# The opening of a block-sparse attention kernel: identity transposes on TensorE between the turns, the masks' flags ahead of the scores, second products chunk by chunk

## The chip, the cores and the metric

The kernel runs on one core of one Trainium2 chip. The metric is the device time of one execution in microseconds (us). Five timed executions of the kernel before took 645.33, 646.21, 646.53, 649.99 and 654.07 us; their median is 646.53 us. The changed kernel is timed against the kernel before on the same chip, and the result is told as a ratio with an interval.

## What is computed

The program is two layers, one after the other. The first is BigBird attention: 4 batches, 8 heads, 768 rows, head dimension 64, in blocks of 32 rows. A query block sees its neighbours, the first and the last block, and three sampled blocks; the queries of the first and the last block see everything. The second is a dropless mixture of experts over the 3072 resulting rows.

```python
scores = scale * np.matmul(q, k.transpose(0, 1, 3, 2))
mask = np.abs(blk_i - blk_j) <= window            # window = 1, in blocks of 32
mask = mask | (blk_i == 0) | (blk_j == 0) | (blk_i == n_blocks - 1) | (blk_j == n_blocks - 1)
for qb in range(n_blocks):
    for kb in sampled_blocks[qb]:
        mask[qb * block:(qb + 1) * block, kb * block:(kb + 1) * block] = True
...
x = attention output, (3072, 512)
expert = argmax(x @ w_gate); y = relu(x @ w1[expert]) @ w2[expert]; out = gate weight * y
```

## The kernel before, in words

All data are float32. The change touches only the opening, before the loop over steps of attention begins (L425 to L436); the rest of the kernel is the same.

**Loads.** SyncE (SP) issues its DMAs in program order. First come eight loads (L293, by `fill_rows`, L146): k and q of batch 0 for the four pairs of heads, each with rows on the partitions. Pairs 0 and 1 land in two staging slots of the tile `room`, pairs 2 and 3 in `kr`. Then come the six 128-row chunks of v (L295, L164). Each chunk that has landed is stored again, all heads of a row side by side, into a DRAM tensor `v_rows` (L297 and L298, L170), because the sampled blocks of v are later gathered from there, row by row.

**Lists.** `make_lists` (L187 to L263) builds small tables from the sampled blocks on GpSimd (POOL) and VectorE (DVE): `spread` and `whose` say which block belongs to which query tile, `own` which half of the partitions counts. At its end TensorE (PE) transposes the identity 22 times into a PSUM tile `idle` that nobody reads (L261 and L262).

**Turns.** `turn_rows` (L148 to L157) brings k or q of one pair into the form that scores need, head dimension on the partitions: 12 transposes of 64x64 on TensorE into a PSUM tile, and then four copies out of it, two on ScalarE (ACT) and two on DVE. `turn_first(pr)` does k and q of one pair, so the opening has eight turns.

**Scores.** `scores_first(pr)` (L422) multiplies the 64 queries of the first and last block with all keys of pair `pr`: 24 products of 64x64 (L351, two matmul records each) and one exponential on ACT (L361).

**Flags and masks.** `make_masks` (L265 to L280) multiplies `spread` and `whose` into a PSUM tile `fl` (four products, L269), from which DVE makes `rows_of` (L270), the row numbers that the gathers read, and four pieces of `mask` (L276).

**Second products.** `attend_all` (L402) multiplies the exponentials with v: for one pair, six chunks and two heads, 12 products into a PSUM bank (L405, by `product`, L385). The order before is pair by pair: pair 0 with chunks 0 to 5, then pair 1, and so on.

**PSUM.** The pool `ps_s` has three buffers of two banks, handed out in rotation to the turns (`tp`), the scores (`s`), `idle` and, before, `fl`. The pool `ps_o` has two buffers of one bank for the second products, one for pairs 0 and 1, one for pairs 2 and 3. A new user of a buffer waits until the last reader of the one before is done.

**Order.** Instructions are issued by hand: on each engine they run in the order in which the code names them. Behind the opening come, before and in the first pass of the loop over steps (L1289 on): `fetch_ends` (SP, reads of `v_rows`, L529), two gathers of v rows (POOL, `fetch_values`, L519, by `rows_of` out of `v_rows`), `place_keys`, `place_middle` and `place_values` (copies on ACT and DVE, L561, L545, L546, L538, L539), the scores of the first two steps (L351, L356), their masks (`masked_two`, L371), and then the second products of the first step (`attend_last`, L407), whose values are in the tile `around` that the gathers and reads fill. SP goes on with the loads of batch 1's k and q into the staging slots (`fill_next`, L140).

The order of the opening before:

```python
    turn_first(0)
    turn_first(1)
    scores_first(0)
    turn_first(2)
    scores_first(1)
    turn_first(3)
    make_masks(*lists)
    make_lists_pool.close()
    scores_first(2)
    scores_first(3)
    for pr in range(NPR):
        attend_all(0, pr, es[("all", pr)], range(NCH))
```

Of the kernel before, what the change touches and what calls it, by code (L numbers as in the profile page):

```python
# [7 lines left out]
F32 = mybir.dt.float32  # L8
# [9 lines left out]
def kernel(  # L18
# [11 lines left out]
    nc = tc.nc  # L30
    P = 128
# [4 lines left out]
    NCH = S // P  # L36
    CW = NCH // 2 * P
    NPR = H // 2
# [32 lines left out]
    ident = const.tile([P, P], F32, name="ident")  # L71
# [12 lines left out]
    ps_o = ctx.enter_context(tc.tile_pool(name="ps_o", bufs=2, space=PSUM))  # L84

    upper, lent = {}, ExitStack()
# [11 lines left out]
    NTI = NB // 2 - 1  # L98
# [49 lines left out]
    def turn_rows(b, pr, which, src):  # L148
        tp = upper["ps_s"].tile([P, 2, 512], F32, name="tp", tag="s")
        for hh in range(2):  # L150
            r = slice(hh * D, (hh + 1) * D)
            for j in range(KG // 2):
                nc.tensor.transpose(tp[:, hh, j * D : (j + 1) * D], src[r, j * P : (j + 1) * P], ident[r, r])
        for hh, copy in enumerate((nc.scalar.copy, nc.vector.tensor_copy)):
            to = sets[b][which][hh * D : (hh + 1) * D, pr, :].rearrange("p (i j a) -> p a i j", j=KG // 2, a=2)
            for a in range(2):
                copy(to[:, a], tp[a * D : (a + 1) * D, hh, : KG // 2 * D].rearrange("p (j i) -> p i j", i=D))  # L157
# [104 lines left out]
            nc.tensor.transpose(idle[:, 0, :P], ident[:], ident[:])  # L262
        return spread, whose, own, qb  # L263

    def make_masks(spread, whose, own, qb):  # L265
        fl = upper["ps_s"].tile([P, 2, 2, NTI], F32, name="fl", tag="s")
        for w in range(2):
            for ch in range(2):
                nc.tensor.matmul(fl[:, w, ch, :], lhsT=spread[:, w, ch, :], rhs=whose[:], start=True, stop=True)  # L269
        nc.vector.tensor_scalar(  # L270
            rows_of.rearrange("p (t c) -> p c t", c=2), fl[:, 0], scalar1=float(BLK), scalar2=qb[:, 2:3], op0=ALU.mult, op1=ALU.add,
        )
        for ch, p0 in ((0, D), (1, 0)):
            for ti in range(2):
                shape = [P - p0, NG - ti, 2, BLK]
                nc.vector.tensor_tensor(  # L276
                    mask[p0:, : NG - ti, 1 + ch, ti, :].rearrange("p t (a i) -> p t a i", a=2),
                    fl[p0:, 1, ch, ti::2].unsqueeze(2).unsqueeze(3).to_broadcast(shape),
                    own[p0:, ch, :].unsqueeze(1).unsqueeze(3).to_broadcast(shape), op=ALU.mult,
                )  # L280
# [9 lines left out]
    for n in range(2 * NPR):  # L290
        pr, which = n // 2, n % 2
# [9 lines left out]
    lists = make_lists(make_lists_pool.enter_context(tc.tile_pool(name="mk", bufs=1)))  # L301
    rt = {}
    xbs, xos, lgs, banks_of, es = {}, {}, {}, {}, {}
# [26 lines left out]
    def plan_all(b, pr):  # L330
        kT = sets[b][0][:, pr, :]
        return [(j, at_cols(kT, c * P + j * D, D), all_queries(b, pr), c * D, D) for c in range(NCH) for j in range(2)], []
# [11 lines left out]
    def scores(*plans):  # L344

        ss = [upper["ps_s"].tile([P, 2, 512], F32, name="s") for _ in plans]
        for s, (few, _) in zip(ss, plans):
            for j, keys, queries, a, n in few:
                for hh in range(2):
                    r = slice(hh * D, (hh + 1) * D)  # L350
                    nc.tensor.matmul(s[j * D : (j + 1) * D, hh, a : a + n], lhsT=keys(r), rhs=queries(r), start=True, stop=True)  # L351
        for s, (_, many) in zip(ss, plans):
            for keys, queries, a, n in many:
                for hh in range(2):
                    r = slice(hh * D, (hh + 1) * D)
                    nc.tensor.matmul(s[:, hh, a : a + n], lhsT=keys(r), rhs=queries(r), start=True, stop=True)  # L356
        found = []
        for s in ss:
            e = ea[:, units[0] % NE, :].rearrange("p (h w) -> p h w", h=2)
            units[0] += 1  # L360
            nc.scalar.activation(e, s[:, :, : 6 * D], AF.Exp, scale=scale)  # L361
            found.append(e)
        return found
# [18 lines left out]
    def product(b, g, pr, ti, hh, e, values, last):  # L382
        bank, begun = bank_of(b, g, pr)
        op = bank[:, : 4 * (D + 4)].rearrange("p (r h w) -> p r h w", r=2, h=2)
        nc.tensor.matmul(  # L385
            op[ti * D : (ti + 1) * D, pr % 2, hh, : D + 1], lhsT=e, rhs=values[:, (2 * pr + hh) * VW : (2 * pr + hh + 1) * VW],
            start=ti not in begun, stop=last, skip_group_check=True,
        )
        begun.add(ti)
# [12 lines left out]
    def attend_all(b, pr, e, chunks):  # L402
        for c in chunks:
            for hh in range(2):
                product(b, GL, pr, 1, hh, e[:, hh, c * D : (c + 1) * D], sets[b][2][:, c, :], c == NCH - 1)  # L405
# [9 lines left out]
            attend_all(b, pr, e_all, range(3, NCH))  # L415


    def turn_first(pr):
        for which in range(2):
            turn_rows(0, pr, which, first[(pr, which)])  # L420

    def scores_first(pr):  # L422
        (es[("all", pr)],) = scores(plan_all(0, pr))

    turn_first(0)  # L425
    turn_first(1)
    scores_first(0)
    turn_first(2)
    scores_first(1)
    turn_first(3)  # L430
    make_masks(*lists)
    make_lists_pool.close()
    scores_first(2)
    scores_first(3)
    for pr in range(NPR):
        attend_all(0, pr, es[("all", pr)], range(NCH))  # L436
    wp = ctx.enter_context(tc.tile_pool(name="wp", bufs=1))
    sm = ctx.enter_context(tc.tile_pool(name="sm", bufs=1))
    work = ctx.enter_context(tc.tile_pool(name="work", bufs=2))
# [864 lines left out]
    for i, (b, g, half) in enumerate(steps):  # L1304
# [15 lines left out]
        if two:  # L1320
            b_, g_, _ = steps[i + 1]
# [245 lines left out]
```

## Time and profile before

| | us |
|---|---|
| median of five timed executions | 646.53 |
| the profiled execution, its own time | 652.5 |
| its span from the first to the last instruction | 650.8 |
| TensorE busy in the span | 616.0 (95%) |
| VectorE busy | 303.7 (47%) |
| ScalarE busy | 223.6 (34%) |
| GpSimd busy | 183.7 (28%) |
| mean granted TensorE clock | 0.965 of full |

Times in the profile count from the start of the span. PE is TensorE's matmul side, PEld its weight loads, DVE VectorE, ACT ScalarE, POOL GpSimd, SP SyncE; a q behind the name is the engine's queue, which issues DMAs. A row of the timeline gives start, duration, engine, line, operation, output<-input and count, and in brackets how long the engine sat idle before it and what ended that. PEclk in a table by stage is the clock that was granted to TensorE, as a share of full speed. The end of a matmul is modelled, so a row's duration reaches some 0.2 us past the time at which the next can start.

The opening and the first steps fill the first 45 of the 650.8 us. In that stretch the granted clock is at half in two spells, 11.47 to 21.71 and 31.95 to 42.19 us.

### The profile page before, as it was taken

What the parts mean: (1) busy time and instruction counts of PE and PEld (TensorE: products, weight loads), DVE (VectorE), ACT (ScalarE), POOL (GpSimd) and SP (SyncE); (2) the same over time, 40 slices, a digit from 0 to 9 for tenths busy, and PEclk for the clock granted to TensorE, in tenths of its full rate; (3) what the DMA queues carried; (4) which work ended last, traced back from release to release, by engine and by line L of the source; (5) the groups of instructions that cost most, each with busy time, mean ns of one, the idle gap of its engine ahead of it and who ended that gap; (6) DMA issues with size and microseconds to landing.
All of it is one profiled execution on the core that took longest, in us unless ns stands there. A gap on an engine that the chain in (4) does not pass through costs nothing. (4 is left out here: it accounts for less than half of the span.)

```text
span 650.8 us, 21378 instructions
## 1 busy us (share of the span) xinstructions
PE 616.0 (95%) x8952; PEld 516.4 (79%) x8952; DVE 303.7 (47%) x978; ACT 223.6 (34%) x430; POOL 183.7 (28%) x288
## 2 busy tenths in 40 slices
PE   7899989989999998899999999999989999999995
PEld 7898889888989887798677777777869678867862
DVE  6547655765667498634920385202091024702200
ACT  5547755765767553431111011111111111111110
POOL 2246733543455244710111221011400212020210
PEclk8879999999999996989999999999999999999998
DMA  9889976896787337966888999869995799989950
GB/s 267 212 179 247 261 187 136 209 263 170 173 194 232 96 107 261 305 235 208 326 307 298 321 382 348 306 227 381 396 398 199 237 406 395 349 277 405 397 190 20
DMA packets 125065, 170.93 MB, mean 263 GB/s; under 512 B 71236, under 2 KB 71237, under 8 KB 124934
## 3 DMA queue, kind: packets, MB, share of 16 engines
q1 hardware_dynamic: 114896, 137.61, 64.9%
q0 software_dynamic: 10000, 31.59, 15.3%
q8 instruction: 80, 1.31, 0.8%
q14 instruction: 51, 0.42, 0.2%
q10 hardware_dynamic: 38, 0.00, 0.0%
HBM read 150.11 MB, written 19.33 MB: 260 GB/s over the span
## 5 line engine op out<-in xcount | busy, mean ns | idle before, releaser
L1127 PEld LDWEIGHTS hp<-around,room 128*128 128x128 f32 x1216 | 138.3, 192 | 7.3 <-issue 5.1
L1127 PE MATMUL hp<-around,room 128*128 128x128 f32 x1216 | 140.8, 276 | 1.4 <-ACT kr L1134 1.4
L1108 DVE STREAM_TRANSPOSE around<-xg 32x128 f32<-32x128 f32 x208 | 62.9, 303 | 126.4 <-PE hp L1127 95.9
L519 POOL DMA_INDIRECT around<-v_rows,rows_of x88 | 96.8, 1100 | 62.7 <-issue 25.2
L361 ACT ACTIVATE ea<-s 128x768 f32<-128x768 f32 x104 | 80.0, 810 | 95.4 <-PE s L356 85.9
L1141 PE MATMUL zp<-room,kr 128*128 128x512 f32 x256 | 112.7, 594 | 0.0
L385 PE MATMUL op<-around,ea 128*64 128x65 f32 x2112 | 92.7, 232 | 11.2 <-DMA around<-v_rows,rows_of 9.2
L385 PEld LDWEIGHTS op<-around,ea 128*64 128x64 f32 x2112 | 80.5, 144 | 20.4 <-DMA around<-v_rows,rows_of 10.7
L1141 PEld LDWEIGHTS zp<-room,kr 128*128 128x128 f32 x256 | 47.5, 190 | 54.6 <-issue 54.6
L367 DVE TENSOR_TENSOR ea<-ea,mask 128x768 f32<-128x768 f32 x80 | 73.3, 955 | 17.4 <-ACT ea L361 16.7
L1134 ACT ACTIVATE kr<-hp 128x512 f32<-128x512 f32 x36 | 21.5, 597 | 117.3 <-PE hp L1127 109.9
L1156 POOL DMA_INDIRECT out_dram<-kr,sB x14 | 14.1, 1006 | 164.9 <-ACT kr L1146 106.1
L1146 ACT ACTIVATE kr<-zp,xg 128x512 f32<-128x512 f32 x16 | 11.0, 687 | 101.2 <-PE zp L1141 101.2
L1234 DVE STREAM_TRANSPOSE ea<-ea 32x128 f32<-32x128 f32 x84 | 21.7, 285 | 32.5 <-DMA ea<-x_rows,gB 31.8
L356 PE MATMUL s<-other,kr 64*128 64x64 f32 x352 | 27.5, 272 | 1.1 <-issue 1.1
L1156 POOL DMA_INDIRECT out_dram<-kr,sA x5 | 5.1, 1019 | 82.8 <-ACT kr L1146 70.6
L356 PE MATMUL s<-room,kr 64*128 64x64 f32 x352 | 26.4, 266 | 0.2 <-issue 0.2
L356 PEld LDWEIGHTS s<-other,kr 64*128 64x128 f32 x352 | 25.6, 201 | 0.0
L356 PE MATMUL s<-other,xk 64*128 64x128 f32 (+1 forms) x192 | 23.3, 320 | 2.4 <-issue 2.4
L351 PE MATMUL s<-room 64*64 64x64 f32 x736 | 24.6, 243 | 0.3 <-DVE room L157 0.3
L356 PEld LDWEIGHTS s<-room,kr 64*128 64x128 f32 x352 | 24.5, 194 | 0.4 <-issue 0.4
L351 PE MATMUL s<-other 64*64 64x64 f32 x736 | 22.5, 228 | 0.4 <-DVE cnA L777 0.4
(344 smaller groups left out, 853.2 us busy)
## 6 DMA issues: line engine op xcount, KB each, us to landing
room<-in_moe_w_dram SPq DMA_DIRECT2D x46, 2048.0 KB
room<-in_moe_w_dram SPq DMA_DIRECT2D x16, 512.0 KB
x_rows<-xb SPq DMA_DIRECT2D x20, 256.0 KB
room<-in_k_dram SPq DMA_DIRECT2D x24, 192.0 KB
room<-in_q_dram SPq DMA_DIRECT2D x24, 192.0 KB
v_rows<-room SPq DMA_DIRECT2D x12, 260.0 KB
v_rows<-other SPq DMA_DIRECT2D x12, 260.0 KB
other<-in_v_dram SPq DMA_DIRECT2D x16, 192.0 KB
```

Of the source, the lines that this page charges most:

```text
L351: nc.tensor.matmul(s[j * D : (j + 1) * D, hh, a : a + n], lhsT=keys(r), rhs=queries(r), start=True, stop=True)
L356: nc.tensor.matmul(s[:, hh, a : a + n], lhsT=keys(r), rhs=queries(r), start=True, stop=True)
L361: nc.scalar.activation(e, s[:, :, : 6 * D], AF.Exp, scale=scale)
L367: nc.vector.tensor_tensor(e, e, m[:, None, :].to_broadcast([P, 2, 6 * D]), op=ALU.mult)
L385: nc.tensor.matmul(op[ti * D : (ti + 1) * D, pr % 2, hh, : D + 1], lhsT=e, rhs=values[:, (2 * pr + hh) * VW : (2 * pr + hh + 1) * VW], sta ...
L519: nc.gpsimd.indirect_dma_start(out=around[p0:, par, 1 + ti + 2 * ch, :], out_offset=None, in_=v_d[b][:, :], in_offset=bass.IndirectOffsetO ...
L1108: nc.vector.transpose(xT[d, :, t], xg[t, :DM].rearrange("p (c q) -> p c q", c=DB)[:, :, d])
L1127: nc.tensor.matmul(hp[:, m, :], lhsT=st[i]["w1"][:, c, fb * P : (fb + 1) * P], rhs=st[i]["xT"][:, c, :], start=(c == 0), stop=(c == DB - 1),)
L1134: nc.scalar.activation(hT[:, g * (FB // 2) : (g + 1) * (FB // 2), :], hp[:], AF.Relu)
L1141: nc.tensor.matmul(zp[:], lhsT=st[i]["hT"][:, fb, :], rhs=st[i]["w2"][:, fb, :], start=(fb == 0), stop=(fb == FB - 1),)
L1156: ins = nc.gpsimd.indirect_dma_start(out=to[:, :], out_offset=bass.IndirectOffsetOnAxis(ap=at, axis=0), in_=rows, in_offset=None, bounds_c ...
L1234: nc.vector.transpose(xT_u[d, :, j * P + tq * 32 : j * P + (tq + 1) * 32], xg_u[t, j, :DM].rearrange("p (c q) -> p c q", c=DB)[:, :, d],)
```

## The change

A function `keep_busy(n)` transposes the 128x128 identity `n` times on TensorE, into a PSUM bank `idle_bank` that nobody reads. It is called behind each of the eight turns, with 2, 3, 11, 4, 4, 4, 4 and 4 transposes, and with 10 between the scores of pairs 2 and 3: 46 in all. The four flag products leave `make_masks` and become `make_flags`, which runs ahead of the first scores and writes into a buffer of `ps_o` and no longer of `ps_s`; DVE makes the masks from it at the same place as before. The second products go chunk by chunk: chunk 0 for all four pairs, then chunk 1, and so on. On ACT, DVE, POOL and SP the same instructions stand in the same order as before; only TensorE's order differs.

```diff
-    def make_masks(spread, whose, own, qb):
-        fl = upper["ps_s"].tile([P, 2, 2, NTI], F32, name="fl", tag="s")
+    def make_flags(spread, whose):
+        fl = ps_o.tile([P, 512], F32, name="op")[:, : 4 * NTI].rearrange("p (w c t) -> p w c t", w=2, c=2)
         for w in range(2):
             for ch in range(2):
                 nc.tensor.matmul(fl[:, w, ch, :], lhsT=spread[:, w, ch, :], rhs=whose[:], start=True, stop=True)
+        return fl
+
+    def make_masks(fl, own, qb):
...
+    idle_bank = ps_o.tile([P, 512], F32, name="op")
+
+    def keep_busy(n):
+
+        for _ in range(n):
+            nc.tensor.transpose(idle_bank[:, :P], ident[:], ident[:])
+
     def turn_first(pr):
         for which in range(2):
             turn_rows(0, pr, which, first[(pr, which)])
+            keep_busy(WHILE[2 * pr + which])
+
+    WHILE = (2, 3, 11, 4, 4, 4, 4, 4)
...
     turn_first(0)
     turn_first(1)
+    flags = make_flags(*lists[:2])
     scores_first(0)
     turn_first(2)
     scores_first(1)
     turn_first(3)
-    make_masks(*lists)
+    make_masks(flags, *lists[2:])
     make_lists_pool.close()
     scores_first(2)
+    keep_busy(10)
     scores_first(3)
-    for pr in range(NPR):
-        attend_all(0, pr, es[("all", pr)], range(NCH))
+    for c in range(NCH):
+        for pr in range(NPR):
+            attend_all(0, pr, es[("all", pr)], (c,))
```

## The prediction, on record before the changed kernel ran

> **What bounds the kernel now.** I read the page first, then the clock by stage, then the timelines of TensorE, GpSimd and SyncE over the first 45 us, because the change touches nothing behind. From the page, two lines:
>
> ```profile
> PE 616.0 (95%) x8952; PEld 516.4 (79%) x8952; DVE 303.7 (47%) x978; ACT 223.6 (34%) x430; POOL 183.7 (28%) x288
> L385 PE MATMUL op<-around,ea 128*64 128x65 f32 x2112 | 92.7, 232 | 11.2 <-DMA around<-v_rows,rows_of 9.2
> ```
>
> TensorE is the busy engine, and most of the little that its second products wait for is a gather of v rows (9.2 of 11.2 us). So a gain in the opening has to show as TensorE starting real work earlier. TensorE's timeline of the opening:
>
> ```profile
> 1.59 4.09 PE L262 MATMUL idle<-ident 128*128 128x128 f32 x22 [1.59 <-POOL ident L73]
> ...
> 8.83 0.74 PE L153 MATMUL tp<-ident,room 64*128 64x64 f32 x12 [0.49 <-DVE room L157]
> 9.88 0.93 PE L351 MATMUL s<-room 64*64 64x64 f32 x48 [0.31 <-DVE room L157]
> ...
> 16.99 1.88 PE L269 MATMUL fl<-whose,spread 24*128 24x11 f32 x8
> 18.79 2.84 PE L351 MATMUL s<-room 64*64 64x64 f32 x96
> 21.56 5.87 PE L385 MATMUL op<-room,ea 128*64 128x65 f32 x96
> ...
> 30.82 0.45 PE L385 MATMUL op<-around,ea 128*64 128x65 f32 x4 [0.53 <-DVE ea L371]
> 32.97 2.43 PE L385 MATMUL op<-around,ea 128*64 128x65 f32 x20 [1.70 <-DMA around<-v_rows,rows_of]
> ```
>
> The last row is the one that decides: with everything of the opening done, TensorE sits idle for 1.70 us, until a gather has landed just before 32.97. What sets that gather's time? GpSimd's timeline, and SyncE's for the stores that it reads behind:
>
> ```profile
> 25.45 1.17 POOL L519 DMA_INDIRECT around<-v_rows,rows_of  x1 [19.66 <-DMA around<-v_rows]
> 26.93 0.93 POOL L519 DMA_INDIRECT around<-v_rows,rows_of  x1 [0.30 <-issue]
> ```
> ```profile
> 16.79 0.43 SPq L164 DMA_DIRECT2D room<-in_v_dram  x1
> 17.86 3.92 SPq L170 DMA_DIRECT2D v_rows<-room  x3
> ```
>
> The gathers are issued at 25.45 and 26.93 behind a wait for DMAs on `v_rows`, whose last stores SyncE issues from 17.86 to 21.78, each when its chunk of v has landed. `rows_of`, the other thing that they need, DVE had ready at 19.69 (L270 starts at 19.44 and takes 0.24). No TensorE instruction is in this chain: loads, v chunks, stores, gathers. Then the clock, by stages that follow its steps (columns: PE, PEld, DVE, ACT, POOL busy, then PEclk):
>
> ```profile
> 4.65:8.06 3.41, 2.56 (x44) 2.29 (x43) 2.76 (x16) 1.59 (x4) 0.98 (x5) 1.00 1.00 306
> 8.06:11.47 3.41, 2.27 (x74) 1.94 (x72) 3.29 (x6) 3.01 (x6) 0.00 (x0) 1.00 1.05 390
> 11.47:14.89 3.42, 3.21 (x71) 2.82 (x68) 2.04 (x5) 2.20 (x5) 0.00 (x0) 0.50 1.21 228
> ...
> 18.30:21.71 3.41, 3.41 (x100) 3.26 (x101) 3.32 (x9) 0.82 (x2) 0.00 (x0) 0.50 1.15 321
> ...
> 28.54:31.95 3.41, 2.20 (x42) 1.78 (x40) 2.14 (x5) 3.01 (x6) 1.14 (x2) 1.00 1.23 256
> 31.95:35.37 3.42, 2.40 (x24) 2.28 (x24) 0.20 (x1) 0.75 (x4) 2.32 (x4) 0.50 1.28 215
> ...
> 38.78:42.19 3.41, 3.41 (x40) 3.29 (x39) 1.92 (x2) 2.20 (x6) 0.01 (x1) 0.50 0.66 169
> 42.19:45.61 3.42, 3.42 (x90) 3.15 (x89) 2.18 (x7) 1.63 (x3) 1.60 (x4) 1.00 0.43 87
> ```
>
> The clock goes to half behind a stage in which TensorE was busy 2.27 of 3.41 us (67%), and again behind one with 2.20 (64%); behind 2.56 (75%) it stayed. Both times it comes back 10.2 us later. The first spell lies under the wait at 32.97; in the second, TensorE has work throughout and pays.
>
> **The change part by part.** Durations are start to start, so the 0.2 us of modelled tail drops out.
>
> *Fillers, 46.* The 22 identity transposes give the price: 14 starts from 1.59 to 4.63 are 217 ns each, those behind it 109 ns. I take 109 ns at full clock, 217 at half, so 5.0 us in all. Five lie before the turn of pair 1's k, which waits for its load until 7.60 anyway: nothing. If that load came earlier, they would cost 0.5.
>
> Do transposes hold the clock up? Row: their spacing halves at 4.63 with nothing but transposes issued before, so they raised it. The Trainium skill ("TensorE: Matmul & The Clock Gate", Part 4) says that the full clock does not engage for transposes, because they do not count as TensorE work in the same way; by it the fillers only cost, and the sum would be that of the second rival, 648.9. The row is of this very instruction, and I follow it.
>
> *Until pair 2's k turn* (11.15 before). Turn of k1 at 7.60 (0.58), 11 fillers (1.20) to 9.38, turn of q1 (0.58), 4 fillers (0.44) to 10.40, flags now here (8 records of 107 ns, half their 213 in the slow stretch: 0.86) to 11.26, scores of pair 0 (0.74) to 12.00. The pauses of 8.83, 9.88 and 11.15 are gone, and this point is 0.85 later.
>
> *From there to the second products* (21.56 before, at half clock). Four turns 2.3, three scores 2.2, 26 fillers 2.8: 19.4. DVE's 16 copies of 557 ns and ACT's of 498 ns with four exponentials of 0.81 keep up, since the fillers fill what they leave. The last exponential ends about 20.4.
>
> *Second products.* A new wait: pair 2's bank held the flags, so its first product waits for DVE's four mask pieces (1.94 us behind the copies, done near 19.9; 21.65 before), and pair 3's for its exponential. Behind them queue all other second products, and behind those the scores of step 0. With some 0.4 us of this and 96 records of 58 ns (5.6) they end at 25.4, against 27.36. If the masks were no earlier than before they would end at 27.3, still not late. Chunk 5 of v, stored from 21.46, is needed near 24.4: no wait; pair by pair it would have been wanted at 20.
>
> *Flags and masks early.* `rows_of` and the masks come some 1.5 us earlier on DVE. Nothing waits for them: the gathers wait for the stores. SyncE's and GpSimd's queues hold the same instructions, and none of those up to the second gather depends on the moved ones. Gathers four and five (32.35, 33.63) may go up to 2 us earlier, queued behind the second; nothing waited for them in the trace. They cost nothing, or, if they slow the second, at most 1.2 us, the spacing of two gathers on their queue (26.93 to 28.16).
>
> *What is late next.* Step 0's scores take 25.4 to 28.3 (2.93 as before), its first second products come 3.46 behind their start, at 28.9, and then TensorE waits for the same gather until 32.97: 3.9 us where it was 1.7. The 2 us saved become waiting. The path's sum: 0.
>
> *The clock behind the wait.* The longer pause puts the clock at half before 32.97 whatever the stages' edges are. Before, the edge was at 31.95; an execution whose edge falls up to 1.9 us behind 32.97 ran that long at full clock and no longer does, which is half of it, 0 to 0.9, and 0.3 on the mean. From both sides: if the second spell went (TensorE arriving so late that it hardly waits), 9.22 us at half would become 4.7, by 60 ns against 118 ns a record of L385 (5.80 us for 96, 2.36 for 20): 4.5 gained. If the before of the timed runs had no such spell and the changed one has, 4.5 lost. I take 0.3, near the row of the profile, in which both have it.
>
> The Trainium skill (same page, "Why this matters for your kernels") asks for no pauses over about 3 us. By it the 1.7 us before are harmless and the 3.9 us are not, and the sum would be 651.0. The row says that 0.53 and 1.70 us close together were enough to lose the clock.
>
> *Sum.* In the profiled execution, 652.5 + 0.3 = 652.8. It stands 6.0 above the median; its 41 us of half clock before 643 are more than every execution need have. On the median, 646.5 + 0.3 = **646.8**.
>
> **Rivals.** *Second spell gone, faster.* If copies or masks hold TensorE so that it arrives at 31 to 32 with the clock up, it keeps it. For: 2 to 3 us of delays would do. Against: the sum is 28.9. Price 4.5: 642.3.
>
> *Fillers at half clock, slower.* If the clock falls at 11.47 all the same, 26 fillers cost 217 ns each, 5.6; with 0.85 from above, less 1.88 for the flags that left the slow stretch, TensorE arrives at 30.82 + 4.6 = 35.4, 2.4 behind the gather: 648.9. It decides from a delay of 2.15 us on, about 15 slow fillers. Against: the pauses that cost the clock are filled. This is the one that says that the change does not do what it does on its face.
>
> *The pause costs the clock that the timed runs before had, slower.* Place 32.97, price up to 4.5: 651.0. For: the profile is 6.0 over the median. Against: in any position of a 3.41 us stage, one holds at least 1.1 us of the two pauses, as the one that lost it did (1.2).
>
> **How the numbers follow.** Forecast 0.72 (644.5 to 648.5 by the scatter of the three middle runs), spell gone 0.06, slow fillers 0.08, clock lost 0.14. The range takes in the last two and most of the scatter, 643.0 to 651.0. A measurement of this kernel tells about 1% from no change: below 640.1 or above 653.0. No case reaches either; I leave 0.04 and 0.06 for what I have not seen, and 0.90 for the same.
>
> **What would show it.** Right: full clock from 11.47 to 21.71, second products starting near 19.4 and ending near 25.4, the gathers issued at 25.4 and 26.9 as before, and a TensorE wait of 3 to 4 us that ends near 32.97 by the gather. Wrong: the first gather issued before 25, which would mean that its wait was for something the change moves; or full clock at 33, or TensorE arriving behind the gather.

## The result, and the profile after

The changed kernel took 651.95 us at the median of 51 executions (641.67 to 660.67), the kernel before 649.99 us at the median of 93 (642.60 to 659.37). That is 1.96 us more, a ratio of 1.0030; the means differ by 1.84 us, with a standard error of 0.58. The ratio, made as for every kernel below, is 1.0002, with a 95% interval of 0.9984 to 1.0021: it takes only the executions within 1.5% of the fastest of their own kernel, 21 of the 51 and 71 of the 93, and the one execution at 641.67 us puts that bar at 651.3 us for the changed kernel, against 652.2 for the kernel before. By either reading there is no gain, and a loss of at most some 0.5%. The profiled execution of the changed kernel took 651.54 us, of which the span is 649.8, at a mean granted clock of 0.976. That clock is higher than the 0.965 of before, and the time is no better. The question is where the clock went.

From the page (busy us, share, instructions; then one costly group; then the queue that brings instructions):

```profile
PE 618.6 (95%) x8998; PEld 517.4 (80%) x8998; DVE 304.0 (47%) x978; ACT 222.9 (34%) x430; POOL 185.4 (29%) x288
...
q8 instruction: 81, 1.33, 0.9%
...
L388 PE MATMUL op<-around,ea 128*64 128x65 f32 x2112 | 92.3, 233 | 8.9 <-DMA around<-v_rows,rows_of 8.1
```

The 46 transposes are there (8998 less 8952). They are 92 instructions, since each matmul has its weight load beside it, and the instruction queue reads one packet more than before (81, before 80). The wait for gathered v rows is 8.1 us over the whole run, where it was 9.2.

TensorE's timeline of the opening (start, duration, engine, line, operation, output<-input, count, and the idle time ahead of it with what ended it):

```profile
8.63 1.42 PE L426 MATMUL op<-ident 128*128 128x128 f32 x11
...
11.27 1.05 PE L269 MATMUL op<-whose,spread 24*128 24x11 f32 x8
12.26 0.93 PE L354 MATMUL s<-room 64*64 64x64 f32 x48
13.12 0.76 PE L153 MATMUL tp<-ident,kr 64*128 64x64 f32 x12
13.81 0.66 PE L426 MATMUL op<-ident 128*128 128x128 f32 x4
14.40 0.77 PE L153 MATMUL tp<-ident,kr 64*128 64x64 f32 x12
...
19.97 1.31 PE L426 MATMUL op<-ident 128*128 128x128 f32 x10
21.21 0.68 PE L354 MATMUL s<-room 64*64 64x64 f32 x29
22.79 0.56 PE L354 MATMUL s<-room 64*64 64x64 f32 x19 [0.90 <-issue]
23.29 6.09 PE L388 MATMUL op<-room,ea 128*64 128x65 f32 x96
...
32.77 0.45 PE L388 MATMUL op<-around,ea 128*64 128x65 f32 x4 [0.53 <-DVE ea L374]
35.93 2.43 PE L388 MATMUL op<-around,ea 128*64 128x65 f32 x20 [2.71 <-DMA around<-v_rows,rows_of]
```

The pauses between the turns are gone, as the change says. But the second products start at 23.29 where they started at 21.56 before, and end at 29.31 where they ended at 27.36. The opening became longer, not shorter. And the row that decides has moved as well: TensorE waits 2.71 us for the gather, until 35.93.

GpSimd's gathers, and SyncE's last stores of v that they wait for:

```profile
28.43 1.17 POOL L535 DMA_INDIRECT around<-v_rows,rows_of  x1 [22.64 <-DMA around<-v_rows]
29.91 0.93 POOL L535 DMA_INDIRECT around<-v_rows,rows_of  x1 [0.31 <-issue]
```
```profile
18.40 4.97 SPq L170 DMA_DIRECT2D v_rows<-room  x3
```

The first gather is issued at 28.43, 2.98 us later than before, because the stores that it follows end at 23.37 and no longer at 21.78, and land later still. Then the clock, by stages that follow its steps (columns: PE, PEld, DVE, ACT and POOL busy, PEclk, share of DMA, GB/s):

```profile
8.23:11.64 3.41, 3.41 (x42) 2.94 (x40) 2.67 (x5) 2.22 (x5) 0.00 (x0) 1.00 1.05 387
11.64:15.06 3.42, 3.42 (x83) 3.06 (x82) 1.18 (x3) 1.85 (x4) 0.00 (x0) 1.00 1.27 240
...
18.47:21.88 3.41, 3.41 (x93) 2.83 (x91) 3.19 (x7) 1.83 (x3) 0.00 (x0) 1.00 1.05 275
21.88:25.30 3.42, 2.46 (x50) 2.24 (x49) 3.31 (x14) 1.22 (x3) 0.00 (x0) 1.00 0.60 184
...
32.12:35.54 3.42, 0.57 (x8) 0.31 (x4) 1.97 (x5) 2.53 (x7) 1.97 (x3) 1.00 1.25 213
35.54:38.95 3.41, 3.02 (x44) 2.91 (x48) 0.49 (x3) 0.00 (x0) 0.98 (x1) 0.50 1.28 215
38.95:42.36 3.41, 3.41 (x78) 3.27 (x71) 2.80 (x8) 2.24 (x4) 1.15 (x2) 1.00 0.69 157
```

The first spell of half clock is gone: PEclk is 1.00 in every stage up to 35.54. Behind the long wait it falls, but for one stage (3.4 us) and not for three (10.2 us).

Counting the matmuls from the end of the run, so that the same one is compared in both traces, the changed kernel is behind by:

```
same matmul, before at     32.97   about 39   about 45   about 63   end
after less before, us      +2.96   +1.57      +0.17      -0.02      -1.0
```

So the 3 us that the opening lost are given back by the shorter spell behind it, and from 45 to 75 us the two kernels run level within 0.7 us. Two effects of 3 us cancel in these two executions. Further on the distance goes to and fro between -4.5 and +2.5 us, as pauses and spells of half clock fall at other places, so the -1.0 at the end is no gain of the opening.

### The profile page after: what moved, and what is told of

It reads as the page before. It is cut to its first block, busy times and chain, and to the rows that moved or that the text cites. A ratio compares the mean times of both kernels' runs of the same rounds, so it can differ in the third digit from the quotient of the medians.

```text
span 649.8 us, 21470 instructions
## 1 busy us (share of the span) xinstructions
PE 618.6 (95%) x8998; PEld 517.4 (80%) x8998; DVE 304.0 (47%) x978; ACT 222.9 (34%) x430; POOL 185.4 (29%) x288
## 5 line engine op out<-in xcount | busy, mean ns | idle before, releaser
L354 PE MATMUL s<-room 64*64 64x64 f32 x736 | 23.2, 230 | 0.9 <-issue 0.9
```

## The experiments

Five chips took part. A is the one of the result. The kernel before took 660.2 us at the median on B, 662.2 on C, 661.8 on D and 648.6 on E, so times are compared on one chip only; each ratio is to the kernel before on its own chip, in the same rounds. All kernels compute the whole reference; added matmuls write a bank that nobody reads.

### Chip B: without fillers, with more, and with the traffic beside the gather held back

`e1_no_fill` is the changed kernel without its 46 transposes; flags and second products stay as changed.

```diff
-            keep_busy(WHILE[2 * pr + which])
...
-    keep_busy(10)
```

> The changed kernel without its 46 filler transposes; flags first and second products chunk by chunk stay. Theory 1 (the gather of v rows sets when TensorE goes on, the opening on TensorE is hidden): ratio to before 1.000 within 0.003; the clock falls to half once between 8 and 13 us, second products start near 20 to 21.5 us, step 0's scores end by 30.5, and TensorE then idles until the second gather has landed, wherever between 32.5 and 36 that is. Rival A (the fillers bring the gather later: it was issued at 28.43 with them and at 25.45 without): the first gather is issued at 25.4 +- 0.5 here. If it is at 27 or later here too, the lateness is scatter of the DMAs and not the fillers. Rival B (the fillers gain by the clock of the first steps): ratio over 1.003.

Measured: 1.0034 (1.0002 to 1.0066), 662.87 us. The clock is at half in two spells before 31 us, 10.51 to 17.3 and 24.16 to 27.6, and not behind it. The first gather is issued at 25.96; TensorE arrives at the first second products of step 0 at 34.35 and resumes at 34.63. So it is the fillers that hold the clock in the opening, and without them the moved flags and the chunk order bring no gain.

`e2_more_fill` has 50 transposes in the last place.

```diff
-    keep_busy(10)
+    keep_busy(50)
```

> The changed kernel with 50 instead of 10 fillers ahead of the last scores: 40 x 109 ns = 4.4 us more TensorE work in the opening. Theory 1: step 0's first second product comes near 32.8 + 4.4 = 37.2 us, behind the gather (33 to 36), so TensorE no longer idles there, the clock stays at full through 31 to 45 us, and what is lost is 1.2 to 4.2 us of position less 0 to 4.5 us of half clock: ratio 0.998 to 1.006, and the waiting row for the gather at that place is gone or under 0.3 us. Rival (the opening on TensorE is the bound): 4.4 us more, ratio 1.007 or over, with no change in the clock behind 31 us.

Measured: 1.0114 (1.0062 to 1.0166), 667.01 us. The clock stays full until 156 us, TensorE arrives at 37.44 and the wait is gone, as in the prediction's first rival (the second spell gone by a late arrival). The kernel is slower all the same, by 0.8% against e1 (their intervals just touch). It arrives 3.1 us later, and it also has the most added instructions of this chip, 172; the run does not tell which of the two it pays for.

`e3_hold_before` and `e4_hold_after` put a store of 8 numbers of `around` ahead of SyncE's loads of batch 1, in the kernel before and in the changed one. SyncE cannot go on until a gather has written them, so the loads no longer run beside it.

```diff
+            if b == 0 and here == 0:
+                nc.sync.dma_start(held_d, around[P - 1 : P, parity(0, GL), 1, :8])
```

> The kernel before, with one tiny store on SyncE that reads the last row of the second gather, put ahead of the loads of batch 1's k and q: SyncE now issues those loads only when the gather has landed, so they no longer share the DMA engines with it. Theory 1: the gathers are issued as before (25.4, 26.9; later if the DMAs are slow) but the second lands 3 to 4 us behind its issue instead of 6.0, near 30 to 31; TensorE waits for it 0 to 0.5 us instead of 1.7, the clock stays at full or falls for one stage only, and 2 to 6 us are gained: ratio 0.991 to 0.997. Rival (position in the opening is given back later, at the next gathers or in the loads held back): first steps earlier by 2 us, ratio within 0.998 to 1.002, with new waits for the held loads at the turns of batch 1 (TensorE row of those turns idle before).

> The changed kernel with the same hold on SyncE's loads. Theory 1: with the gather no longer late, TensorE's own opening sets the end: it arrives at 32.8 us here against 30.8 in the held kernel before, so this one is 1 to 2.5 us slower than that, or equal where the held kernel before still loses the clock once: ratio to before 0.993 to 0.999. Rival (the fillers keep the clock and so win once the gather is out of the way): faster than the held kernel before by over 0.3%.

Measured: e3 1.0039 (1.0003 to 1.0075), 661.80 us; e4 1.0107 (1.0066 to 1.0147), 666.86 us. In e3 the second gather is issued at 27.72 and has landed by 30.85, when the held store goes out: 3.1 us, where it took 6.0 in the profile of before (26.93 to 32.97, on chip A). So the loads beside it do slow the gather. To hold them back brought nothing, because TensorE arrived at 32.62 only and resumed at 33.11, and both spells of half clock were still there (from 11.26 and from 31.74, 10.2 us each). In e4 the gather is issued at 28.10, TensorE arrives at 34.44, and the clock is at half from 34.99 for 3.4 us. "The wait for the gather sets the end" is not true in any of the four traces of this chip; the kernel before without the hold has no trace here.

### Chip C: both kernels again, the same filling in fewer instructions, and filling ahead of the wait

`c1_before` and `c2_after` are the two kernels as they are.

> The kernel before, unchanged, as an experiment of its own: ratio 1.000 within its interval, which says how far two identical kernels can seem to differ here. Its trace shows how much the first gather's issue scatters without fillers. Theory 2, formed from the first four traces (first gather issued at 28.4, 27.5 and 28.1 us with fillers, at 25.5, 26.0 and 26.2 without): the fillers make the DMAs late; here it comes at 25.3 to 26.3 us. Rival (scatter of the DMAs): over 27 here.

> The changed kernel, unchanged, once more. Theory 2: first gather issued at 27.5 to 28.5 us, and the second products start at 23 us or later, 1.5 to 2.5 us behind those of before on the same chip. Ratio 0.998 to 1.006. Rival (scatter of the DMAs): first gather issued under 26.5.

Measured: c1 0.9983 (0.9956 to 1.0011), 660.99 us; c2 1.0059 (1.0032 to 1.0087), 665.02 us. On this chip the change costs 3.9 us (0.0059 of 662). That is twice the 1.96 of chip A, but the means of all executions on A give 1.0011 to 1.0046, which this interval overlaps, so it is not shown that the two chips differ. The timelines show that the loss is not the first gather. TensorE in c1, then GpSimd and TensorE in c2:

```profile
22.83 6.32 PE L385 MATMUL op<-room,ea 128*64 128x65 f32 x96
33.57 1.62 PE L385 MATMUL op<-around,ea 128*64 128x65 f32 x24 [0.53 <-DVE ea L371]
```
```profile
25.49 1.17 POOL L535 DMA_INDIRECT around<-v_rows,rows_of  x1 [19.70 <-DMA around<-v_rows]
```
```profile
34.08 1.62 PE L388 MATMUL op<-around,ea 128*64 128x65 f32 x24 [0.53 <-DVE ea L374]
```

In both kernels the 24 second products now stand in one row: TensorE arrives so late (33.57 and 34.08) that there is no wait of note for the gather (0.28 us in each). In c2 the first gather goes at 25.49, as early as in the profile of before: "the fillers always make the gather late" falls. And the clock of c2 is full through the whole opening, while c1 has 13.65 us at half from 10.29, and still c2 arrives 0.5 us later. The loss comes further on. Against c1, by the same matmul, c2 is behind by 0.40 us at 58, 0.43 at 77, 4.58 at 161 and 3.93 at 641: 4.15 us between 77 and 161. Two rows of c2 in that stretch:

```profile
87.35 0.62 PE L388 MATMUL op<-around,ea 128*64 128x65 f32 x13 [0.99 <-DMA around<-v_rows,rows_of]
...
92.11 0.21 PE L359 MATMUL s<-other,xk 64*128 64x64 f32 x1 [1.31 <-issue]
```

The waits of TensorE from 84 to 93 us, first in c1 and then in c2 (line, releaser: us in total, times, longest):

```profile
PE s L351 <- issue: 0.4, 1, 0.4
```
```profile
PE s L359 <- issue: 1.3, 1, 1.3
PE op L388 <- DMA around<-v_rows,rows_of: 1.0, 1, 1.0
```

One is a gather that lands late, the other is "issue": nothing that the profile shows, which would fit a wait for the instruction itself, though no run shows that. These 1.9 us are about half of the 4.15.

`f1_long_fill` fills the same pauses with 18 long matmuls of the identity (128 to 512 moving columns), 36 instructions in place of 92.

```diff
-        for _ in range(n):
-            nc.tensor.transpose(idle_bank[:, :P], ident[:], ident[:])
+        for n in times:
+            to = idle_bank[:, : n * P].rearrange("p (a b) -> p a b", a=n)
+            nc.tensor.matmul(to, lhsT=ident[:], rhs=ident[:, None, :].to_broadcast([P, n, P]), start=True, stop=True)
...
-    WHILE = (2, 3, 11, 4, 4, 4, 4, 4)
+    WHILE = ((), (2,), (4, 2), (2,), (), (4,), (), (4,))
...
-    keep_busy(10)
+    keep_busy(4, 1)
```

> The changed kernel with the same 5 us of filling done by 9 float32 products of the identity with 128 to 512 moving columns: 36 instructions (weight loads counted) instead of 92. Theory 2a (the fillers' instructions have to be fetched by the same DMA engines as v, and a fetch falls on a chunk of v that the others wait for): first gather back at 25.3 to 26.5 us, clock at full through the opening as with the short fillers. Rival 2b (TensorE's activity itself, its reads of SBUF beside the DMAs' writes, makes the DMAs late): first gather at 27.5 to 28.5 us as with the short fillers.

Measured: 1.0017 (0.9986 to 1.0048), 662.53 us. Gather at 25.26, arrival at 32.91, the only half clock of the opening from 32.63 (3.4 us), and between 77 and 161 us it loses 0.3 us against c1. The median is 2.5 us under that of c2 (the intervals overlap), and the clock gained is worth nothing that can be told here either.

`g1_fill_wait` is the kernel before with 18 identity transposes ahead of the first second products of step 0, where TensorE waited in the profile.

```diff
+            if i == 1:
+                idle_s = upper["ps_s"].tile([P, 2, 512], F32, name="idle_s", tag="s")
+                for _ in range(18):
+                    nc.tensor.transpose(idle_s[:, 0, :P], ident[:], ident[:])
```

> The kernel before with 18 identity transposes (18 x 109 ns = 2.0 us) only where TensorE waits for the gather, behind the scores of step 1 and ahead of the first second products of step 0. Theory 1 (that wait is idle time, and the half clock behind it is what it costs): the 2.0 us fit into the 2.2 us of pauses, TensorE goes on when the gather has landed as before, no second spell of half clock near 32 to 42 us, ratio 0.993 to 0.998. Rival (the gather is not late in most executions, so fillers delay TensorE by up to 2 us and save no clock): ratio 1.000 to 1.003.

Measured: 1.0006 (0.9973 to 1.0039), 662.87 us. The transposes run from 32.26 to 36.0, and the clock is at half from 32.69 for 3.4 us, in place of 10.2 as in the profile of before. But the first spell, in an opening that is that of the kernel before, lasts 3.4 us too in this trace (from 19.04), so the shorter spell cannot be put to the transposes. Nothing is gained.

### Chip D: the number of instructions alone

`h1_count_only` is the kernel before with 46 transposes of 32x32 behind the two turns of pair 0: 92 instructions, and only 1.4 us of TensorE's time (7.83 to 9.27).

```diff
+    idle_bank = ps_o.tile([P, 512], F32, name="op")
     turn_first(0)
+    for _ in range(46):
+        nc.tensor.transpose(idle_bank[:32, :32], ident[:32, :32], ident[:32, :32])
```

> The kernel before with 46 transposes of a 32x32 corner of the identity behind the second turn, where TensorE waits for a load: 92 instructions more, as in the change, with under 3 us of work and nothing else of the change. Theory 3 (formed from the traces so far: on the slower chips the changed kernel loses its 3 to 4 us not in the opening but between 81 and 165 us, at pauses of 1.3 to 1.75 us ended by no semaphore, always at the same instruction, 7124 matmuls from the end; 92 more instructions ahead move the places at which TensorE's instructions are fetched): the pause of over 1 us at that instruction appears here too, and the ratio is like the changed kernel's on the same chip, within 0.003. Rival (the loss is of the fillers' work or of the new order of the opening): no pause over 0.6 us there, ratio under 1.002.

`i1_neutral_fill` is f1 with the 22 idle transposes of `make_lists` as two long matmuls, so that it has about as many TensorE instructions as the kernel before (8950, before 8952).

```diff
-        for c in range(22):
-            nc.tensor.transpose(idle[:, 0, :P], ident[:], ident[:])
+        to = idle[:, 0, :].rearrange("p (a b) -> p a b", a=4)
+        for c in range(2):
+            nc.tensor.matmul(to, lhsT=ident[:], rhs=ident[:, None, :].to_broadcast([P, 4, P]), start=True, stop=True)
```

> The changed kernel with its fillers as 9 longer products (36 instructions) and the 22 identity transposes at the start as 2 longer products (8 instructions instead of 44): exactly as many TensorE instructions as before, the clock held up as in the change. Theory 3: the pauses behind the opening lie where they lie in the kernel before, none over 1 us at 7124 from the end; the end of the opening comes 0.5 to 1.5 us earlier than before and that is kept: ratio 0.996 to 1.001. Rival (the change costs by its fillers' time): ratio 1.003 or over.

`k1_fill_only` is the kernel before with the 46 fillers alone; `c3_after` is the changed kernel.

```diff
+            keep_busy(WHILE[2 * pr + which])
...
+    keep_busy(10)
```

> The kernel before with the change's 46 fillers alone; flags and second products in the old place and order. Theory 3: the same pause of 1.3 us or more at 7124 from the end, ratio within 0.003 of the changed kernel's on the same chip. Rival (the new place of the flags and the order chunk by chunk carry the loss): ratio under 1.002.

> The changed kernel once more, to compare with the three others on one chip. Theory 3: pauses of over 1 us at 7124 and of some 1 us at 7268 from the end, as in its two other traces; ratio 1.000 on a chip like the first (650 us), 1.004 to 1.007 on chips like the two others (660 us).

Measured: h1 1.0069 (1.0038 to 1.0100), 666.74 us; i1 1.0009 (0.9970 to 1.0048), 662.34; k1 1.0041 (1.0011 to 1.0072), 664.58; c3 1.0074 (1.0035 to 1.0112), 666.42. So 92 instructions that fill nothing cost here as much as the whole change, and the same filling without them costs nothing that can be told: i1 lies 4.1 us under c3, though their intervals still overlap. In h1's timeline of TensorE:

```profile
7.83 1.51 PE L428 MATMUL op<-ident 32*32 32x32 f32 x46
...
34.34 0.60 PE L385 MATMUL op<-around,ea 128*64 128x65 f32 x4 [0.52 <-DVE ea L371]
36.32 2.43 PE L385 MATMUL op<-around,ea 128*64 128x65 f32 x20 [1.38 <-DMA around<-v_rows,rows_of]
```

and its first gather:

```profile
27.53 1.17 POOL L522 DMA_INDIRECT around<-v_rows,rows_of  x1 [21.74 <-DMA around<-v_rows]
```

The 46 transposes touch nothing of the gather's chain, and yet the gather goes at 27.53 (25.45 in the profile of before, 25.85 in c1, both on other chips) and TensorE resumes at 36.32. i1 has a late gather as well (27.07), though it has no more instructions than before; what its fillers shift is when they run.

Against c1 (for the kernels of B and D too, whose kernel before takes about as long as that of C), by the same matmul, the kernels lose between 77 and 161 us:

```
92 or more added TensorE instructions:  c2 4.15  c3 3.59  e4 3.59  k1 5.82  h1 2.08  e2 2.02
none to 36 added:                       e1 0.45  f1 0.30  i1 0.13  g1 -0.12  e3 -0.13
```

The split is clean on chips B, C and D, but each number is one execution, and the stretch was chosen on c2. On chip A after loses only 0.4 us against before there, with the same 92 instructions; and i1 loses 3.0 us between 58 and 70 instead, under half clock from 59.20 for 6.8 us. The loss does not sit in one fixed "issue" pause: at the same matmul, 7124 from the end, after, e4, c2 and k1 have one (1.75, 1.75, 1.31 and 1.07 us), h1 and c3 have none, and before has one of 1.52 at another place. Nor is it the sum of these pauses: from 77 to 161 us TensorE has 3.2 us of "issue" in c1, 3.7 in c2 and 2.0 in h1. The waits for gathered v rows differ more: 0 in c1, 1.7 in c2, 1.6 in c3, 2.5 in e4 and 1.4 in h1. On chip A they are 3.0 in before already, and 2.7 in after. Why they grow with the added instructions on the other chips is open.

### Chip E: more instructions that do nothing

`n0_before` is the kernel before; n1 and n2 are h1 with 64 and 128 transposes of 32x32, that is 128 and 256 instructions.

```diff
+    for _ in range(64):
+        nc.tensor.transpose(idle_bank[:32, :32], ident[:32, :32], ident[:32, :32])
```

> The kernel before, unchanged, for its trace on the same chip as the next two: first fetch of 16 KB behind 12 us starts under 13.1 us, first gather issued under 26.6, no loss between 81 and 165 us against its earlier trace (within 0.6 us).

> The kernel before with 64 transposes of a 32x32 corner of the identity behind the second turn: 128 instructions more, 1.9 us of work, half of a 16 KB read if an instruction takes 64 bytes (1.31 MB in 80 reads for 17,904 matmuls and weight loads and some thousand others). Theory 3 (position against the reads): against the kernel before on the same chip it falls back by 2 us or more between 81 and 165 us; ratio 1.003 to 1.009. Rival (mere number): as much as 92 instructions cost times 1.4, 4 to 6 us in that stretch.

> The same with 128 such transposes: 256 instructions more, 3.7 us of work, one whole 16 KB read. Theory 3 (position against the reads): the pauses behind the opening lie as in the kernel before, and between 81 and 165 us it falls back by less than 1 us; the ratio is what the 1 to 3 us of opening cost, 1.001 to 1.005. Rival (mere number): it falls back by 6 us or more in that stretch, ratio over 1.008.

Measured: n0 652.32 us in one execution; n1 1.0044 (1.0009 to 1.0080), 651.38; n2 1.0034 (1.0000 to 1.0069), 650.44. Count alone costs on this chip too (n2's interval only just), and whether twice the count costs more these intervals do not tell. The loss is not where it was on the other three: n1 is 6.5 us behind n0 at 58 already (a gather wait of 2.48 us until 35.90, and half clock from 34.43 for 10.2 us), and gains 0.5 between 77 and 161; n2 gains 2.0 there. What the instructions cost is not one pause at one place.

n2 also bears on the clock. Its 32x32 transposes run from 6.51 to 10.35, and turns follow:

```profile
7.72:11.13 3.41, 3.41 (x114) 3.36 (x111) 1.79 (x4) 0.58 (x2) 0.00 (x0) 1.00 1.05 405
11.13:14.54 3.41, 2.67 (x62) 2.25 (x60) 2.23 (x4) 2.28 (x5) 0.00 (x0) 0.50 1.10 217
```

TensorE is busy for the whole stage, and the clock falls to half behind it all the same. In after, a stage of 128x128 transposes and turns (8.23 to 11.64) kept it. So in this one trace the small transposes did not hold the clock, although the profile counts them as busy.

## Why the prediction was right and wrong

That the change gains nothing was right. The predicted time was not: the median lies 0.95 us above the range.

**The base failed.** The step is "On the median, 646.5 + 0.3 = 646.8", with "It stands 6.0 above the median". Five executions gave 646.53; 93 give 649.99, and only 10 of them lie below 646.53. So 3.5 of the 5.2 us between forecast and median are the base's. The profiled 652.5 was 2.5 above the kernel's median and no odd execution. "The scatter of the three middle runs" went from 646.21 to 649.99, so nearly all of it lay above the forecast; the prediction laid its width around 646.5, as 644.5 to 648.5. With 649.99 as the base and the same 0.3 the forecast would have been 650.3.

**The 0.3 for the change: too small.** The other 1.7 us are the change's own, as far as the scatter tells: the medians differ by 1.96 us, the means by 1.84 with a standard error of 0.58. Which stretch carries them on chip A the two traces do not tell, since there the changed kernel ends 1.0 us ahead.

**The clock in the opening: right.** "The pauses that cost the clock are filled" holds in every trace with fillers: no half clock between 8 and 31 us in after, c2, c3, e2, e4 and k1, and two spells in e1, which has none. The Trainium skill ("TensorE: Matmul & The Clock Gate", Part 4) says that transposes do not raise the clock; the stages at 1.00 above, filled by transposes of the identity, contradict it for transposes of 128x128. The 32x32 transposes of n2 agree with the page.

**"From there to the second products … 19.4": wrong by 3.9 us.** The fillers were priced at 109 ns each, back to back. 1.1 us were lost before pair 2's k (13.12, forecast 12.00), 0.34 of them by the five fillers priced at "nothing": the turn of pair 1's k starts at 7.94 and not at 7.60, with no wait ahead of it. From there to the second products it took 10.17 us where 7.4 were forecast. Start to start, a turn with fillers behind it takes 0.69 us (0.58 forecast), four fillers 0.59 (0.44), the scores of a pair 0.86 (0.74), the ten fillers 1.24 (1.09). So each change from one kind of TensorE instruction to another cost 0.1 to 0.15 us in this trace, and the fillers stand in nine places. Four turns, three scores, four groups of four and the ten make 0.44 + 0.36 + 0.60 + 0.15 = 1.55 us, the "issue" pause at 22.79 0.90, together 2.45 of the 2.77. The rest is open, and so is what the "issue" pause waits for: k1 has one of 1.68 us at the same place, c2 none.

**"The gathers issued at 25.4 and 26.9 as before": wrong in this trace.** "No TensorE instruction is in this chain: loads, v chunks, stores, gathers" is true of its waits and false of its transfers. In the traces of after, c3, e2, e4, h1 and i1 the gather goes at 27.07 to 28.43, and there the instruction queue's read of 16 KB that lies behind 12 us begins at 13.18 to 14.10; in before, c1, n0, e1, e3, g1, f1, c2 and k1 it begins at 12.76 to 13.08, and the gather goes at 25.26 to 26.59. In the late ones the last of the fifth v chunk's 16 parts lands 0.4 to 2.1 us behind the fifteenth, in the early ones 0.01 to 0.23. The profile's page counts instruction reads and the loads of v on the same 16 DMA engines, and when the read falls differs with what TensorE is given to run. That fits fifteen traces, but no run moved this read alone, and n1 and n2 (reads at 11.74 and 10.85, gathers at 26.81 and 27.21, fifth chunk 0.69 and 1.29) lie outside the pattern of the reads: argued, not shown.

**The new wait for the masks: small, as forecast.** "Some 0.4 us of this" was taken; none shows in after, 0.80 us in e1, and in c2 the row is

```profile
24.17 4.54 PE L388 MATMUL op<-room,ea 128*64 128x65 f32 x71 [0.40 <-DVE mask L279]
```

But "`rows_of` and the masks come some 1.5 us earlier on DVE" was wrong. In after they come 1.4 us later (`rows_of` starts at 20.84, before at 19.44), and the masks are ready at 23.06 where 19.9 was forecast:

```profile
20.84 0.24 DVE L273 TENSOR_SCALAR rows_of<-op,qb 128x22 int32<-128x22 f32 x1
21.12 1.94 DVE L279 TENSOR_TENSOR mask<-op,own 64x384 bf16<-64x384 f32 x4
```

It cost nothing in after, since the second products started only at 23.29.

**"TensorE waits for the same gather until 32.97: 3.9 us":** it waited 2.71, until 35.93, since both the first of these second products (28.9 forecast, 32.77 measured) and the landing moved. In the two other traces of the kernel before, c1 and n0, there is no such wait. It comes and goes with the execution: h1, c3 and n1 have 1.38, 1.69 and 2.48 us of it.

**The clock behind the wait: +0.3, measured −2.8** (from +2.96 at the resume to +0.17 at 45 us). "The longer pause puts the clock at half before 32.97" did not come: it was full until 35.54, and "full clock at 33" was one of the prediction's own signs of being wrong. The forecast also let the second spell end as before; it lasted one stage in place of three. That the two profiled executions stand 0.17 us apart at 45 us, near the 0.3 forecast, is because this stands against the 3.0 of the late gather, and both were unforeseen: luck.

**On other chips the term is larger still.** 1.0059 on C and 1.0074 on D are 4 to 5 us. h1 on the one side, f1 and i1 on the other point to the 92 added instructions for most of it; the intervals of f1 and i1 still overlap those of c2 and c3. The flags and the chunk order are not free of suspicion: e1, which has them without fillers, stands at 1.0034 on B. No rival named the instructions themselves. Whether chip A pays less than C and D is not shown. How the cost falls stays open: total "issue" pauses of TensorE are 5.8 us in before and 4.7 in after on chip A and 7.7 to 15.5 in the traces of B, C and D, but on C the kernel before has more of them (13.4 in c1) than the changed one (12.8 in c2).

No version beat the kernel before: the lowest ratios were g1 (1.0006) and i1 (1.0009), and c1, the kernel before against itself, gave 0.9983.

## What to carry to other kernels

Keeping the clock is not yet a gain: c2 ran its whole opening at full clock, c1 13.65 us of it at half, and c2 arrived 0.5 us later. The fillers must be counted as work: at their own time, with 0.1 to 0.15 us for each switch of kind, and with what added instructions cost by themselves (1.0069 in h1). Where a pause must be filled, few long instructions look better than many short ones: the same cover in 36 and not 92 instructions stood at 1.0017 where the other stood at 1.0059, though the intervals overlap. And before a wait of the profile is priced, look whether a second execution has it, and take the base from more than five times if they spread over 1%.

## What the runs showed of the hardware

- The same kernel took 648.6 to 662.2 us at the median on five chips. For this change the ratio was 1.0030 by the medians on A, 1.0059 on C and 1.0074 on D; whether the chip makes the difference is not shown.
- 92 TensorE instructions that compute nothing of use and take 1.4 us of it cost 1.0069 (1.0038 to 1.0100) in h1, and 256 of them 1.0034 (1.0000 to 1.0069) in n2, on another chip: the price did not grow with the number.
- Half clock comes in whole stages of 3.41 us, one to four of them in these traces (3.4, 6.8, 10.2 and 13.65 us). The busy time of the stage ahead does not decide: the clock fell behind stages busy 2.20 and 2.27 us (in before), 2.93 (at 29.28 in g1) and 3.41 (at 7.72 in n2, small transposes), and stayed behind 2.46 (at 21.88 in after) and 1.58 (at 479.1 in before). The Trainium skill's rule (same page, "Why this matters for your kernels"), no pauses over about 3 us, is too mild: 1.21 us of pauses within one stage (busy 2.20 of 3.41, in before) were enough. How many stages a spell lasts is open: one behind 2.85 us idle in after, three behind 1.21 in before.
- A gather of v rows landed 3.1 us behind its issue with SyncE's loads held back (e3), and 6.0 to 7.6 beside them (26.93 to 32.97 in before, 29.91 to 35.93 in after, 28.29 to 35.90 in n1).
